# Linear attention and a mixture of experts in fp32: queries and folded projection as further groups of the experts' loop

## The chip, the cores and the metric

One core of a Trainium2 chip runs the kernel. The metric is the device time of one execution in microseconds (us), the median of the runs shown. The engines are PE (TensorE matmuls; PEld is its weight load), DVE (VectorE), ACT (ScalarE), POOL (GpSimd) and SP (SyncE, which here only issues DMAs). PSUM, where matmuls accumulate, has 8 banks of 128 x 512 fp32; SBUF holds tiles of 128 partitions. In the profile, L12 is line 12 of the kernel's own file.

## The reference

2048 tokens x of width D = 512. All weights are fp32. Two branches of the same tokens are mixed by a gate for each token:

```python
phi = lambda t: jnp.where(t > 0, t + 1, jnp.exp(t)) + 1e-6
pq, pk = phi(q), phi(k)                        # q, k, v = x @ wqkv, H = 32 heads of 16
kv = jnp.einsum("bhsd,bhse->bhde", pk, v)      # one 16 x 16 state for each head
z = jnp.einsum("bhsd->bhd", pk)
num = jnp.einsum("bhqd,bhde->bhqe", pq, kv)
den = jnp.einsum("bhqd,bhd->bhq", pq, z)[..., None] + 1e-6
a = (num / den).transpose(0, 2, 1, 3).reshape(B, S, D) @ wo
...
h = _silu(x @ w1[e]) @ w2[e]                   # for each of 8 experts, F = 1792
b = b + w[e] * h                               # w: softmax gates; top 8 of 8, so all
g = sigmoid((x * gate_w).sum(-1, keepdims=True))
out = g * a + (1 - g) * b
```

Nearly all work is the experts' two layers over all tokens.

## The kernel before, in words

**Precision.** Each fp32 product is made of three matmuls in a rounded fp32 format (F32R): `mm3` (L57) multiplies high by high, high by low and low by high. So each operand is split: ACT copies the high part, DVE subtracts to get the low part.

**Seven products.** Both layers of the experts are multiplied as 2 x 2 blocks with 7 block products in place of 8 (`ORDER`, L103: P1, P7, P2, P4, P6, P5, P3). This needs sums of blocks: of the weights (`prep`, L132, steps 0 to 7), of the tokens (`x_sums`, L384, by DVE subtractions) and of the hidden values (`differ`, DVE). The tokens are taken in two halves of 1024.

**Weights.** `m.groups` (L99) lists the groups: half, expert, pair of blocks of F. `load` fetches a group by DMAs on SP's queue; `prep` splits and sums it in steps dealt out over the seven steps of the group ahead of it. In the first half of the tokens, the second layer's weights are prepared too and written to DRAM (`w2stash`), from where both halves read them.

**Attention** (`attention`, L211) stands ahead of the experts' loop.
1. For each tile of 128 tokens: `g_proj` multiplies the tokens by the keys' weights with the gates' columns; ACT and DVE form phi (`g_done`, L353); a DMA on POOL's queue adds phi's rows to one tile in SBUF (`pks`); `y_acc` (L375) accumulates phi(k)^T x over all tokens in four PSUM banks. Since v = x Wv, the state is that sum times Wv. In the last of these tiles the token sums of the second half are made (L384) and written to DRAM (`xstash`), later loaded for the second half by `x_next`.
2. `q_proj` (L480) forms the queries, 12 matmuls for each of 16 blocks of 128 columns by 512 tokens, `state` (L567) the heads' states, `normaliser` (L552) the sums of keys, `fold` (L590) multiplies the state by wo, so that the projection of a query block is one product with the folded weights. `q_sums` (L501), `q_rec` and `q_norm` (L520) divide by the denominators; `a_out` (L534) does the folded projection, 192 matmuls, scales by the token gate and writes the rows to DRAM (`astash`). Twelve query matmuls stand between the last two tiles' `y_acc`.

**The experts' loop** (`experts`, L685). The order is written out by hand: each engine executes in the order in which the code issues, and each step u of the loop issues a share of every stream. `up` (L727) is six matmuls of the first layer, seven steps for a group; `mid` calls `tick` (L898), six matmuls of the second layer for step n = u - LAG, LAG = 44 steps behind; `other` does the splits of hidden values (`high` on ACT, `low_h` on DVE), `differ` and the weights' `prep`. `load_w2` fetches the stashed second-layer weights, 512 KB for two ticks, on SP's queue. `evict` (L875) takes finished PSUM banks, `finish` (L863) multiplies by the token's expert weight and adds it to a sum in DRAM (`acct`) by an accumulating DMA on POOL's queue. Rows of the first half are transposed during the second half (`rows_first`, L929), with the attention's rows added; those of the second half at the end (`turn_some`, `end`), from tiles that `load_tail` and `load_att` fetch on POOL's queue.

Tiles come from pools with tags and numbers of buffers. A new tile waits until the last use of the buffer that it takes is over. Pools that are closed hand their memory to later ones in the same way.

Of the kernel before, what the change touches and what calls it, by code (L numbers as in the profile page):

```python
# [42 lines left out]
def gated_mix_kernel(ctx: ExitStack, tc: tile.TileContext, xT, x, wk, wv, wqkv_q, wo, wm, out):  # L43
# [18 lines left out]
    def act_copy(dst, src):  # L62
        nc.scalar.activation(dst, src, AF.Copy)  # L63
# [7 lines left out]
    m.wgt = const.tile([P, NT, E], F32, name="wgt")  # L71
    m.gat = const.tile([P, NT], F32, name="gat")
    m.mx = const.tile([P, NT], F32, name="mx")
# [7 lines left out]
    m.X = {}  # L81
    for tb, K in ((1, 0), (2, 0), (2, 1), (3, 0), (0, 0), (0, 1), (1, 1), (3, 1)):
        m.X[tb, K] = [x_tile(f"x{tb}{K}{c}", "xs" if (tb, K) == (3, 1) else "x") for c in "hl"]
    m.XO = [[None] * 7, [None] * 7]
    m.xstash = dram.tile([7, 2, P, 2 * TB], F32, name="xstash")
    m.astash = dram.tile([NT, P, D], F32, name="astash")
    m.w2stash = [dram.tile([P, 2, D], F32, name=f"w2stash{i}") for i in range(E * NPAIR * 7 // 2)]
    m.wgtd = dram.tile([E, S], F32, name="wgtd")
    m.acct = dram.tile([2, 2, KT, P, TB], F32, name="acct")

    weights(m)
    attention(m)
    experts(m)

def weights(m):
    nc, v, w1p, act_copy = m.nc, m.v, m.w1p, m.act_copy
    m.groups = [(p, e, q) for p in range(2) for e in range(E) for q in range(NPAIR)]  # L99
    m.NG = len(m.groups)  # L100
    m.NG0 = m.NG // 2
# [7 lines left out]
    def raw_tile(name):  # L109
        return w1p.tile([P, 2048], F32, name=name, tag="rm", bufs=2)  # L110

    def load(g):
        if g >= m.NG:
            return
        p, e, q = m.groups[g]
        src = m.wm[e * NPAIR + q]
        r = raw[g] = raw_tile(f"rm{g}").rearrange("p (r h w f) -> p r h w f", r=2, h=2, w=2)
        for i in range(2):
            nc.sync.dma_start(r[:, i, :, 0, :], src[:, i, :D].rearrange("p (h f) -> p h f", h=2))
        if p == 0:  # L120
            for i in range(2):
                nc.sync.dma_start(r[:, :, i, 1, :], src[:, i, D:].rearrange("p (h f) -> p h f", h=2))
# [9 lines left out]
    def prep(g, step):  # L132
        if g >= m.NG:
            return
        p, e, q = m.groups[g]
        r = raw[g]
        both = p == 0
# [15 lines left out]

        def high2(n, src):
            if both:
                act_copy(two(ws_tile(n), 0), src)

        def low2(n, src, *prods):
            if both:
                w = ws.pop((g, n))  # L160
                v.tensor_sub(two(w, 1), src, f32(two(w, 0)))  # L161
                for half, prod in enumerate(prods):
                    i = (e * 7 + m.ORDER.index(prod)) * NPAIR + q
                    nc.sync.dma_start(m.w2stash[i // 2][:, i % 2].rearrange("p (c f) -> p c f", c=2),
                                      f32(w[:, :, half * HALF:(half + 1) * HALF]))
# [7 lines left out]
        elif step == 1:  # L173
# [6 lines left out]
            high2(1, r[:, :, 1, 1])  # L180
        elif step == 2:
            o = ops[g][6][0]
            v.tensor_sub(o[:, 1], r[:, 1, 1, 0], f32(o[:, 0]))  # L183
            if both:
                w = ws.pop((g, 0))
                v.tensor_sub(w[:, 1, :HALF], r[:, 0, 0, 1], f32(w[:, 0, :HALF]))
                i = (e * 7 + m.ORDER.index("P1")) * NPAIR + q
                nc.sync.dma_start(m.w2stash[i // 2][:, i % 2].rearrange("p (c f) -> p c f", c=2), f32(w[:, :, :HALF]))
        elif step == 3:
            low2(1, r[:, :, 1, 1], "P2", "P4")  # L190
# [6 lines left out]
        elif step == 5:  # L197
            low(5, r[:, 1, :, 0])
            high2(2, r[:, :, 0, 1])
        elif step == 6:  # L200
            low2(2, r[:, :, 0, 1], "P6", "P7")
            high(3, r[:, 0, :, 0], (3, 0), (4, HALF))
            high2(3, r[:, :, 1, 1])
        else:
            low(3, r[:, 0, :, 0])
            low2(3, r[:, :, 1, 1], "P3", "P5")
# [4 lines left out]
def attention(m):  # L211
    nc, tc, v, mm3, act_copy, X, XO = m.nc, m.tc, m.v, m.mm3, m.act_copy, m.X, m.XO
    xT, x, wk, wv, wgt, gat, mx, x_tile = m.xT, m.x, m.wk, m.wv, m.wgt, m.gat, m.mx, m.x_tile
    ctx = ExitStack()
    att = ctx.enter_context(tc.tile_pool(name="att", bufs=1))
    wpool = ctx.enter_context(tc.tile_pool(name="wpool", bufs=4))
    hid = ctx.enter_context(tc.tile_pool(name="hid", bufs=1))
# [14 lines left out]

    def xk(c, tb, k, lo=0, hi=TB):
        return X[tb, k // 2][c][:, k % 2, lo:hi]

    scr = att.tile([P, 8, TB], F32, name="scr")
    yT = scr[:, :KT]
    kvt = scr[:, 7, :].rearrange("p (k f) -> p k f", k=KT)

    zc = att.tile([P, KT, 2, NH], F32R, name="zc")  # L240
    zf = att.tile([P, KT, NH], F32, name="zf")
    mask = att.tile([P, P], F32, name="mask")
    maskh = att.tile([P, KT, NH], F32, name="maskh")
    spread = att.tile([P, KT, P], F32R, name="spread")
    rhs = att.tile([P, 2, TB], F32R, name="rhs")
    pks = att.tile([P, D], F32, name="pks")
    ones = att.tile([P, NH], F32, name="ones")
    lg = att.tile([P, NT, NL], F32, name="lg")

    def sf_tile(name):  # L250
        return hid.tile([P, TB], F32, name=name, tag="sf", bufs=4)


    def hl_tile(name, dt=F32R):
        return hid.tile([P, 2, TB], dt, name=name, tag="hl", bufs=6)

    def o_tile(name):
        return m.w1p.tile([P, 2, TB], F32R, name=name, tag="o", bufs=4)

    def w_tile(name, width=2048):  # L260
        return wpool.tile([P, 8 * G[1]], F32R, name=name, tag="w")[:, :width]
# [4 lines left out]
    def load_raw(name, src):  # L266
        r = m.raw_tile(name)
        nc.sync.dma_start(r, src)
        return four(r)

    raw = {}

    def load_x(tb):
        if tb < 3:
            raw[tb] = load_raw(f"x{tb}", xT[tb])
        else:
            raw[tb] = scr[:, :KT]
            nc.sync.dma_start(raw[tb], four(xT[tb]))

    def split_x(tb, k):  # L280
        split(raw[tb][:, k, :], xk(0, tb, k), xk(1, tb, k))


    g0 = w_tile("g0").rearrange("p (c k f) -> p c k f", c=2, k=KT)
    g1 = w_tile("g1", 8 * G[1]).rearrange("p (c k f) -> p c k f", c=2, k=KT)
    gw = (g0, g1)
    x0 = four(m.raw_tile("x0"))
    r0 = four(m.raw_tile("r0")[:, :KT * G[0]])
    r1 = [hl_tile(f"r1{i}", F32) for i in range(2)]
    for k in range(KT):  # L290
        nc.sync.dma_start(x0[:, k, :], xT[0][:, k * TB:(k + 1) * TB])
        nc.sync.dma_start(r0[:, k, :], wk[:, k * G[0]:(k + 1) * G[0]])
    for i in range(2):
        at = KT * G[0] + 2 * i * G[1]
        nc.sync.dma_start(r1[i][:, :, :G[1]], wk[:, at:at + 2 * G[1]].rearrange("p (k f) -> p k f", k=2))
# [8 lines left out]
    def load_xt(tb):  # L304
        xr[tb] = m.raw_tile(f"xr{tb}").rearrange("p (t d) -> p t d", d=D)
        nc.sync.dma_start(xr[tb], x[tb * TB:(tb + 1) * TB, :].rearrange("(t p) d -> p t d", p=P))

    def split_xt(t):
        xt[t] = o_tile(f"xt{t}")
# [13 lines left out]
    band(maskh, [[P, KT], [-DH, NH]], 1)  # L323
    sp = sf_tile("sp")[:NH, :].rearrange("p (c f) -> p c f", c=KT)
    band(sp, [[P, KT], [1, P]], -DH)
    for i in range(2):
        act_copy(spread[i * NH:(i + 1) * NH], sp)
    for t in (spread, rhs):
        nc.gpsimd.memset(f32(t)[2 * NH:], 0.0)

    def phi(dst, ps):
        nc.scalar.activation(dst, ps, AF.Exp)
        nc.scalar.activation(ps, ps, AF.Relu)
        v.scalar_tensor_tensor(dst, dst, 1.0, ps, op0=ALU.min, op1=ALU.add)

    def eps_high(h, d):
        nc.scalar.activation(h, d, AF.Copy, bias=EPS)  # L340

    def eps_low(lo, d, h):
        v.scalar_tensor_tensor(lo, d, EPS, f32(h), op0=ALU.add, op1=ALU.subtract)
# [9 lines left out]
    def g_done(t, g, ps):  # L353
        if g == 0:
            pk[t] = sf_tile(f"pk{t}"), hl_tile(f"pkh{t}")
            phi(pk[t][0][:, :G[0]], ps)
        else:
            d, h = pk[t]
            phi(d[:, G[0]:], ps[:, :D - G[0]])
            eps_high(h[:, 0], d)  # L360
            eps_low(h[:, 1], d, h[:, 0])
# [22 lines left out]
    def x_sums(p, step):  # L384
        a, b = raw[2 * p], raw[2 * p + 1]
        b11, b21, b12, b22 = a[:, :2], a[:, 2:], b[:, :2], b[:, 2:]
        if step == 0:
            v.tensor_sub(b11, b12, b11)
        elif step == 1:
            v.tensor_sub(b12, b22, b12)  # L390
        elif step == 2:
            v.tensor_sub(b22, b22, b11)
        elif step == 3:
            v.tensor_sub(b21, b21, b22)
        else:
            n, low = divmod(step - 4, 2)
            i, r = ((3, b22), (5, b12), (1, b11), (6, b21))[n]
            if not low:
                if p == 0:
                    XO[0][i] = [x_tile(f"t{i}{c}") for c in "hl"]  # L400
                else:
                    tmp[i] = hl_tile(f"t{i}h"), hl_tile(f"t{i}l")
                act_copy((tmp[i] if p else XO[0][i])[0], r)
            else:
                h, lo = tmp[i] if p else XO[0][i]
                v.tensor_sub(lo, r, f32(h))
                if p:
                    for c, t in enumerate((h, lo)):
                        nc.sync.dma_start(m.xstash[{1: 3, 3: 4, 5: 5, 6: 6}[i], c], f32(t).rearrange("p k t -> p (k t)"))

    tmp = {}

    def x_high(p, n):
# [677 lines left out]
```

## Time and profile before

| | |
|---|---|
| median of 3 runs | 2371.43 us (2370.62 to 2373.01) |
| profiled execution | 2370.8 us |
| its span, first to last instruction | 2369.1 us |
| granted PE clock, mean | 1.000 |
| PE busy | 2347.2 us, 10530 instructions |
| DVE busy | 1783.0 us |
| ACT busy | 1381.8 us |
| POOL busy | 129.6 us |
| DMA | 489.76 MB, mean 207 GB/s |

A busy time is the time in which an engine executed something, and the share is of the span. A chain of waits follows the work back from the last instruction to what released it; an engine with nearly all of this chain is what bounds the kernel. Groups of instructions read "out<-in": the tile written and the tiles read, then the count, busy time, mean ns of one, and the idle time ahead of them with what ended it. Windows give the busy time of each engine in a stretch of the run; a DMA share of 1.00 means that all 16 engines moved data throughout.

### The profile page before, as it was taken

What the parts mean: (1) busy time and instruction counts of PE and PEld (TensorE: products, weight loads), DVE (VectorE), ACT (ScalarE), POOL (GpSimd) and SP (SyncE); (2) the same over time, 40 slices, a digit from 0 to 9 for tenths busy, and PEclk for the clock granted to TensorE, in tenths of its full rate; (3) what the DMA queues carried; (4) which work ended last, traced back from release to release, by engine and by line L of the source; (5) the groups of instructions that cost most, each with busy time, mean ns of one, the idle gap of its engine ahead of it and who ended that gap; (6) DMA issues with size and microseconds to landing.
All of it is one profiled execution on the core that took longest, in us unless ns stands there. A gap on an engine that the chain in (4) does not pass through costs nothing.

```text
span 2369.1 us, 31088 instructions
## 1 busy us (share of the span) xinstructions
PE 2347.2 (99%) x10530; PEld 1939.8 (82%) x10530; DVE 1783.0 (75%) x3023; ACT 1381.8 (58%) x2594; POOL 129.6 (5%) x175
## 2 busy tenths in 40 slices
PE   9999999999999999999999999999999999999998
PEld 8877788888888888888888888888888888888886
DVE  5687888888888888888876667766766667676667
ACT  5556766666666666666655555555555555555553
POOL 2101000000000000000000000000000000000011
PEclk9999999999999999999999999999999999999999
DMA  6626988898888988888894544555454645454456
GB/s 183 212 86 203 307 270 266 265 269 262 270 275 259 285 261 263 271 265 267 270 322 136 157 152 162 165 159 170 143 148 132 165 137 140 150 139 150 139 171 224
DMA packets 297936, 489.76 MB, mean 207 GB/s; under 512 B 22640, under 2 KB 214256, under 8 KB 296880
## 3 DMA queue, kind: packets, MB, share of 16 engines
q1 hardware_dynamic: 278192, 450.99, 57.2%
q0 software_dynamic: 19584, 36.78, 9.2%
q8 instruction: 83, 1.36, 0.2%
q14 instruction: 77, 0.63, 0.1%
HBM read 332.42 MB, written 151.06 MB: 204 GB/s over the span
## 4 chain that ended last, share of the span: by engine, by line
PE 95%; DVE 2%; DMA 2%; ACT 1%; issue 0%; SPq 0%; DVEq 0%; ACTq 0%
PE p L58 15%; PE p L60 15%; PE p L59 15%; PE a L58 9%; PE a L60 9%; PE a L59 9%; PE c L60 4%; PE c L58 4%; PE c L59 4%; PE b L58 2%; PE b L59 2%; PE b L60 2%; PE g L350 1%; PE q L488 1%; PE q L485 1%; PE q L486 1%
## 5 line engine op out<-in xcount | busy, mean ns | idle before, releaser
L58 PE MATMUL p<-ho,w 128*128 128x512 f32 x1568 | 611.2, 390 | 3.6 <-issue 1.8
L60 PE MATMUL p<-ho,w 128*128 128x512 f32 x1568 | 610.1, 389 | 0.0
L59 PE MATMUL p<-ho,w 128*128 128x512 f32 x1568 | 610.0, 389 | 0.0
L836 DVE TENSOR_TENSOR ho<-s,ho 128x512 fp32r<-128x512 f32 x784 | 536.2, 685 | 62.8 <-ACT ho L63 60.5
L63 ACT ACTIVATE ho<-s 128x512 fp32r<-128x512 f32 x784 | 485.7, 621 | 18.0 <-DVE s L817 10.8
L58 PEld LDWEIGHTS p<-ho,w 128*128 128x128 f32 x1568 | 294.3, 188 | 67.2 <-issue 2.2
L60 PEld LDWEIGHTS p<-ho,w 128*128 128x128 f32 x1568 | 294.3, 188 | 61.2
L59 PEld LDWEIGHTS p<-ho,w 128*128 128x128 f32 x1568 | 294.4, 188 | 60.9
L63 ACT ACTIVATE o<-rm 128x512 fp32r<-128x512 f32 x448 | 255.0, 569 | 148.2 <-PE a L60 126.5
L717 ACT ACTIVATE s<-s 128x512 f32<-128x512 f32 x224 | 141.3, 631 | 280.5 <-DVE s L776 207.6
L147 DVE TENSOR_TENSOR o<-rm,o 128x512 fp32r<-128x512 f32 x336 | 230.2, 685 | 16.4 <-ACT o L63 16.1
L776 DVE TENSOR_TENSOR s<-c,s 128x512 f32<-128x512 f32 x112 | 77.3, 690 | 168.1 <-PE c L60 166.2
L63 ACT ACTIVATE ws<-rm 128x512 fp32r<-128x512 f32 (+1 forms) x209 | 117.9, 571 | 65.6 <-DMA w2stash<-ws 54.2
L783 DVE TENSOR_TENSOR s<-a,s 128x512 f32<-128x512 f32 x112 | 77.4, 691 | 73.2 <-PE a L60 72.5
L717 ACT ACTIVATE s<-b 128x512 f32<-128x512 f32 x112 | 67.1, 599 | 110.0 <-PE b L60 96.7
L63 ACT ACTIVATE s<-a 128x512 f32<-128x512 f32 x112 | 66.8, 596 | 93.2 <-PE a L60 93.2
L161 DVE TENSOR_TENSOR ws<-rm,ws 128x512 fp32r<-128x512 f32 x158 | 108.1, 684 | 3.2 <-ACT ws L63 3.2
L183 DVE TENSOR_TENSOR o<-rm,o 128x256 fp32r<-128x256 f32 x112 | 47.1, 421 | 66.0 <-ACT o L63 66.0
L870 POOL DMA_DIRECT2D acct<-c x28 | 24.0, 856 | 1074.9 <-DVE c L866 650.0
L63 ACT ACTIVATE s<-c 128x512 f32<-128x512 f32 x112 | 66.6, 595 | 26.8 <-PE c L60 26.7
L63 ACT ACTIVATE b<-a 128x512 f32<-128x512 f32 x112 | 64.8, 579 | 21.1 <-PE a L60 21.1
L815 DVE TENSOR_TENSOR s<-s,s 128x512 f32<-128x512 f32 x112 | 76.7, 685 | 0.0
(343 smaller groups left out, 4431.9 us busy)
## 6 DMA issues: line engine op xcount, KB each, us to landing
w<-w2stash SPq DMA_DIRECT2D x392, 512.0 KB, 4.3
w2stash<-ws SPq DMA_DIRECT2D x367, 256.0 KB, 4.7
rm<-wm SPq DMA_DIRECT2D x336, 256.0 KB, 4.9
wb<-wgtd SPq DMA_DIRECT2D x16, 512.0 KB, 5.8
acct<-c POOLq DMA_DIRECT2D x28, 256.0 KB, 5.0
acct<-d POOLq DMA_DIRECT2D x28, 256.0 KB, 5.4
acct<-k POOLq DMA_DIRECT2D x26, 256.0 KB, 5.3
acct<-e POOLq DMA_DIRECT2D x26, 256.0 KB, 5.9
```

Of the source, the lines that this page charges most:

```text
L58: nc.tensor.matmul(ps, wh, xh, start=start, stop=False, skip_group_check=True)
L59: nc.tensor.matmul(ps, wh, xl, start=False, stop=False, skip_group_check=True)
L60: nc.tensor.matmul(ps, wlo, xh, start=False, stop=stop, skip_group_check=True)
L63: nc.scalar.activation(dst, src, AF.Copy)
L147: v.tensor_sub(two(o, 1), src, f32(two(o, 0)))
L161: v.tensor_sub(two(w, 1), src, f32(two(w, 0)))
L183: v.tensor_sub(o[:, 1], r[:, 1, 1, 0], f32(o[:, 0]))
L717: nc.scalar.activation(dst, src, AF.Silu)
L776: v.tensor_add(sn[g, 2], bank[g, "c"], sn[g, 2])
L783: v.tensor_add(sn[g, 3], bank[g, "a"], sn[g, 3])
L815: v.tensor_sub(t21, t21, t11)
L836: v.tensor_sub(h[:, 1], s, f32(h[:, 0]))
```

## The change

The queries and the folded projection leave the stage ahead of the loop and become two more "parts" of the loop, one for each half of the tokens, both by 7 products.

- `parts` lists 8 experts and a query part (`e == E`, 2 pairs of blocks) for each half. In the first layer the two halves' query groups (four groups) stand between the first half's and the second half's expert groups; `hidden` (L544) applies phi to their results and writes them to DRAM (`pqd`). In the second layer the query parts come last: 28 further ticks.
- The stage of attention becomes `keys` (L249): keys, `y_acc` and token sums only. The state, the fold, gates and normaliser are done in the first 12 steps of the loop; the folded weights, normaliser and gates go through DRAM.
- The queries are normalised during the second half of the loop, a block of 512 tokens every 49 ticks (`queries_load`, `queries_first`, `queries_last`), in which the token gate is multiplied in.
- Before the query parts, the sums of the experts are loaded from DRAM (`load_sums`, POOL's queue) and the parts' results are added to them by DVE (`evict`); all 16 row tiles are then transposed in the tail. No rows of the attention are stored any more.
- The token sums are made by ACT negating a block in place and a DMA on POOL's queue that accumulates another block onto it, SBUF to SBUF, 512 KB each (`x_sum`). They are spread over tiles 3 to 15. Three split token blocks of the second half are written to DRAM at tile 11 (`x_keep`), and the first group's weights are loaded and prepared at tiles 11 to 15.
- Second-half ticks start 28 steps later than before against the steps of the loop (`LAG1`), so that 28 steps have the first layer alone.

```diff
+    m.parts = [SimpleNamespace(e=e, h=h, n=NPAIR) for h in range(2) for e in range(E)]
+    m.parts += [SimpleNamespace(e=E, h=h, n=2) for h in range(2)]
...
+    for i in (*range(E), 2 * E, 2 * E + 1, *range(E, 2 * E)):
...
-    def x_sums(p, step):
+    def x_sum(p, step):
         a, b = raw[2 * p], raw[2 * p + 1]
         b11, b21, b12, b22 = a[:, :2], a[:, 2:], b[:, :2], b[:, 2:]
-        if step == 0:
-            v.tensor_sub(b11, b12, b11)
...
+        dst, src = ((b11, b12), (b12, b22), (b22, b11), (b21, b22))[step]
+        if step < 3:
+            act_copy(dst, dst, scale=-1.0)
+        nc.gpsimd.dma_start(dst, src, accum_op=ALU.add)
+
+    def x_part(p, i):
...
+        if p == 0:
+            h, lo = XO[0][i] = [m.x_tile(f"t{i}{c}") for c in "hl"]
+        else:
+            both = room(f"t{i}", F32R).rearrange("p (c k f) -> p c k f", c=2, k=2)
+            h, lo = both[:, 0], both[:, 1]
...
+        if p:
+            for c, t in enumerate((h, lo)):
+                nc.sync.dma_start(m.xstash[i, c], f32(t).rearrange("p k t -> p (k t)"))
...
+        if t in (4, 8, 11):
+            load_xt((t + 1) // 4)
...
+        if t in (11, 12):
+            m.load(t - 11)
...
         y_acc(t - 1)
...
+        for p, at in ((0, t), (1, t - 6)):
+            if at in (4, 6, 7):
+                x_sum(p, at // 2 - 1 if at < 7 else 3)
+            if at in (4, 6, 8, 9):
+                x_part(p, {4: 1, 6: 5, 8: 3, 9: 6}[at])
+        if t == 8:
+            x_sum(1, 0)
+        if t == 11:
+            x_keep(0, (2, 0)), x_keep(2, (2, 1)), x_keep(4, (3, 1))
+        if t > 11:
+            m.prep(0, 2 * t - 24), m.prep(0, 2 * t - 23)
     y_acc(NT - 1)
...
+    def hidden(g, f, t, dst, src):
+        part, q = groups[g]
+        if part.e < E:
+            nc.scalar.activation(dst, src, AF.Silu)
+            raw[g, f, t] = dst
+            return
+        if dst is src:
+            dst = r_tile(f"e{g}_{f}{t}")
+        phi(dst, src)
+        nc.sync.dma_start(m.pqd[part.h, t, 2 * q + f], dst)
...
+    LAG = 44
+    LAG1 = LAG + 28
...
+        if part.e == E:
...
+            if prod != "P1":
+                s = sums[part.h, r * 2 + sub, j]
...
+                v.tensor_add(s, src, s)
...
+    def drain():
+        m.yT, m.wvs, m.wos = ([r_tile(f"{n}{k}") for k in range(KT)] for n in ("yT", "wv", "wo"))
+        for k in range(KT):
+            nc.sync.dma_start(m.wvs[k], m.wv[:, k * D:(k + 1) * D])
...
+    def load_sums(h, j):
+        for dt in range(KT):
+            if dt % 2 == 0:
+                r = m.xpool.tile([P, 2, TB], F32, name=f"tl{h}{j}{dt}", tag="x", bufs=14)
+            sums[h, dt, j] = r[:, dt % 2]
+            nc.gpsimd.dma_start(r[:, dt % 2], m.acct[h, j, dt])
...
+        if u == 1:
+            state()
+        if u in (3, 4, 5, 6):
+            fold(u - 3)
...
+        at = n - END
+        if -22 <= at < -14:
+            load_query(0, at + 22)
+        if -8 <= at < 0:
+            load_query(1, at + 8)
+        if at in (-12, -10):
+            load_sums(0, (at + 12) // 2)
+        if at in (3, 5):
+            load_sums(1, (at - 3) // 2)
+        if 11 <= at < 15:
+            rows(0, at - 11)
+        if 16 <= at < 20:
+            rows(0, NTT + at - 16)
+        if 24 <= at < 28:
+            rows(1, at - 24)
```

869 lines of the change are left out of this document (383 added, 486 removed).

## The prediction

> **What bounds the kernel now.** I read the page's busy shares and its chain first, then PE's waits, then the busy time of each engine in stretches of the run.
>
> ```profile
> span 2369.1 us, 31088 instructions
> PE 2347.2 (99%) x10530; PEld 1939.8 (82%) x10530; DVE 1783.0 (75%) x3023; ACT 1381.8 (58%) x2594; POOL 129.6 (5%) x175
> PE 95%; DVE 2%; DMA 2%; ACT 1%; issue 0%; SPq 0%; DVEq 0%; ACTq 0%
> PE a L58 <- ACT hl L63: 3.2, 4, 2.2
> PE a L58 <- ACT s L63: 1.9, 2, 1.2
> ```
>
> PE is busy 99% of the span and carries 95% of the chain. The waits (total us, times, longest) are single events: 3.2 us in the folded projection, which the change removes, and 1.9 us where the loop starts. So a change pays only by fewer PE instructions, and costs wherever PE has to wait. The stretches say where a wait is near (length, then PE, PEld, DVE, ACT, POOL busy, PE clock, share of the 16 DMA engines, GB/s):
>
> ```profile
> 27.00:95.00 68.00, 68.00 (x432) 61.52 (x431) 38.00 (x75) 36.47 (x82) 10.83 (x13) 1.00 0.55 153
> 61.00:64.00 3.00, 3.00 (x26) 2.91 (x25) 2.27 (x5) 2.16 (x5) 0.85 (x1) 1.00 0.49 87
> 97.00:116.00 19.00, 19.00 (x100) 15.41 (x99) 11.79 (x26) 9.42 (x17) 0.62 (x1) 1.00 1.00 358
> 225.00:300.00 75.00, 72.85 (x319) 59.33 (x318) 66.63 (x112) 56.49 (x111) 2.98 (x7) 1.00 0.93 306
> 400.00:600.00 200.00, 200.00 (x884) 165.62 (x883) 168.51 (x280) 128.80 (x245) 7.72 (x9) 1.00 0.86 267
> 2325.00:2334.00 9.00, 9.00 (x41) 7.47 (x40) 5.21 (x9) 3.89 (x7) 0.00 (x0) 1.00 1.02 407
> ```
>
> In the keys' stage (27 to 95 us) PE never waits, with the DMA engines at 0.55. In the first half of the loop (400 to 600) they are at 0.86, DVE at 168.51/200 = 84%. At 97 to 116 us and in the tail, transfers fill them (358 GB/s at 1.00, 407 at 1.02). DMA is the second resource, and this change adds DMA just where it is scarce.
>
> **The change part by part.** The clock is 1.00 throughout, so one row prices a matmul.
>
> ```profile
> 27.10 0.28 PE L350 MATMUL g<-g,x10h 128*128 128x256 f32 x1
> 32.81 0.40 PE L350 MATMUL g<-g,x10h 128*128 128x256 f32 x2
> 95.33 0.39 PE L60 MATMUL y<-pkh,xt 128*128 128x512 f32 x1
> 212.06 0.39 PE L58 MATMUL a<-x00h,o 128*128 128x512 f32 x1
> 1298.02 0.39 PE L58 MATMUL a<-n0h,o 128*128 128x512 f32 x1
> 1317.06 0.39 PE L58 MATMUL a<-n0h,o 128*128 128x512 f32 x1
> 104.02 3.77 PE kv L572 x32
> 107.79 0.81 PE z L555 x8
> 114.22 3.44 PE wp L594 x8
> ```
>
> Two groups of the loop start 1317.06 - 1298.02 = 19.04 us apart and hold 84 matmuls: 0.2267 us each. One token tile of the keys' stage takes 32.81 - 27.10 = 5.71 us.
>
> *A, the arithmetic.* Queries (12 matmuls for each of 16 blocks) and folded projection (192) are 384 matmuls; as 7 products of 8 they are 336, that is 48 x 0.2267 = 10.9 us less. I price the whole stage, since its waits go with it. From the end of the last matmul of tile 14 at 95.56 (95.33 plus one cadence) to the loop at 212.06 are 116.5 us. In its place stand the last tile's 12 matmuls (2.7 us), the state, normaliser and fold (3.77 + 0.81 + 3.44 = 8.0 us) and 336 + 32 + 16 = 384 matmuls x 0.2267 = 87.1 us (the 32 sums over heads and 16 spreads are kept): 97.8. So A = -18.7 us, if nothing waits.
>
> *B, the end of the keys' stage.* Before, tile 15 was covered by query products that PE could do meanwhile, and the six stash copies were issued behind it. Now the queue of SP holds, from tile 10 on, in order: t1 (2 x 512 KB), tokens (1 MB), the first weights (4 x 256 KB), six copies of 512 KB (x_keep, line 439 of the changed kernel), the second weights, t5 (2 x 512 KB), and only then what t3 waits for. These are 12 units of 512 KB and 8 of 256 KB: 16 x 512 KB.
>
> ```profile
> pks<-pk POOLq DMA_DIRECT2D x16, 256.0 KB, 3.3
> xstash<-t3h SPq DMA_DIRECT2D x1, 512.0 KB, 2.7
> xstash<-x20h SPq DMA_DIRECT2D x1, 512.0 KB, 10.7
> xstash<-x31l SPq DMA_DIRECT2D x1, 512.0 KB, 12.5
> x<-xT SPq DMA_DIRECT2D x4, 256.0 KB, 4.3
> w<-w2stash SPq DMA_DIRECT2D x392, 512.0 KB, 4.3
> 97.50 0.32 SPq L409 DMA_DIRECT2D xstash<-t5l  x1
> L340 ACT ACTIVATE pkh<-pk 128x512 fp32r<-128x512 f32 x16 | 10.1, 633 | 9.3 <-DVE pk L337 9.3
> L343 DVE SCALAR_TENSOR_TENSOR pkh<-pk,pkh 128x512 fp32r<-128x512 f32 x16 | 11.1, 692 | 11.2 <-ACT pkh L340 11.2
> L335 ACT ACTIVATE pk<-g 128x256 f32<-128x256 f32 x32 | 12.2, 380 | 20.2 <-issue 9.4 <-PE g L350 9.4 <-ACT t3h L63 0.9
> L63 ACT ACTIVATE xt<-xr 128x512 fp32r<-128x512 f32 x16 | 9.9, 620 | 3.3 <-DMA xr<-x 3.3
> L337 DVE SCALAR_TENSOR_TENSOR pk<-pk,g 128x256 f32<-128x256 f32 x32 | 13.2, 419 | 17.7 <-ACT g L336 17.6
> L63 ACT ACTIVATE t3h<-x 128x1024 fp32r<-128x1024 f32 x1 | 1.0, 1043 | 0.0
> ```
>
> At 407 GB/s at share 1.02, 512 KB hold the engines 1.31 us, at 358 GB/s 1.46 us: 21 to 23.4 us for 16. An accumulation inside SBUF isn't shown at 512 KB; the nearest row is pks (256 KB): around one of them the engines are at 0.49 for 3 us, 1.47 us, so 2.9 us at 512 KB. Two token sums and three pks in that stretch add 5.9 + 4.4. The Trainium skill, DMA: Bandwidth & Descriptors, section Anatomy of one DMA — SWDGE (gpsimd) path, fits 2.0 us plus bytes/436e3 for such a DMA, so by that page the moving part of 512 KB would be an estimated 1.2 us; the row of pks doesn't bear that out, and with it the case is the one called *free* below.
>
> Counted from the start of tile 10 the queue fills at 8.0 us (t1 is ready in tile 11, at 5.71 plus some 2.3 of its ACT and DVE work), so t5 lands at 39.2 to 41.7. ACT takes its work in order: t3h waits for that landing (its room is t5's; x_part, line 421 of the changed kernel), and behind it stand two preparations of the first weights, exp and relu of tile 15 (4 x 0.38), its high part (0.63), its low part on DVE (0.69) and xt: 1.04 + 2 x 0.62 + 1.52 + 0.42 + 0.63 + 0.69, some 6 us with the hand-overs. PE gets tile 15 at 45.3 to 47.7 where it was due at 6 x 5.71 = 34.2: 11 to 13.5 us. xt of tiles 12 to 14 reuse the room of three of the copied tiles, and such copies landed after 10.7 to 12.5 us before; what PE loses there is part of the same queue. I take B = +13. Low end: nothing queues, and tile 15 follows tile 14 with no query product between, 1.3 us of the phi chain and 1.7 of the copies' landing, +3. High end: 358 GB/s and landing latency on top, +17.
>
> *C, the state.* Its weights wv (4 x 256 KB, drain, line 760 of the changed kernel) are loaded into memory that opens with the last matmul of tile 15. PE has only 7 matmuls (1.6 us) before the product at step 1, and 256 KB take 4.3 us to land (row of x<-xT): 2.7 us late, plus four issues on SP of 0.32 us or more each, behind stashes: +4.5, from 2 to 7. Behind the state's first matmul PE's whole queue stands, and ACT and DVE have nothing of the loop to do until it moves.
>
> *D, the first steps of the loop.* Gates, wo, the folded weights' way through DRAM now stand here, and the engines were at 0.93 with 2.15 us of PE idle in 225 to 300. +1 (0 to 5).
>
> *E, the last parts.* 28 more ticks of 1.36 us (6 x 0.2267) each need half a 512 KB load, 0.66 us of the engines. On POOL's queue from the last expert's sixth product on stand 6 accumulations (256 KB, 1.47 us by pks, 1.8 with read and write in DRAM as I estimate it) and 26 loads of 256 KB (0.66): 28 us of work at the 0.7 us per tick that SP's loads leave, 40 ticks. They start near tick 768, so the last lands near 808, and the second half's sums are wanted at tick 800, with some 4 ticks of slack from PSUM. +3 (-1 to +8); the tail before was late too.
>
> *F, the end.* Before, four DVE additions closed the kernel; now copies, shared by ACT and DVE.
>
> ```profile
> 2362.70 2.48 DVE L951 TENSOR_TENSOR at<-o,at 128x512 f32<-128x512 f32 x4 [0.42 <-PE o L957]
> 2342.50 3.10 DVE L836 TENSOR_TENSOR ho<-s,ho 128x512 fp32r<-128x512 f32 x5 [0.78 <-ACT ho L63]
> L717 ACT ACT_TABLE_LOAD x1 | 1.3, 1283 | 0.0
> ```
>
> Half of 2.48, and a bit of the way: -1.5 (-2 to 0).
>
> *G, the four added groups and the queries' blocks.* Three more DVE operations of 0.62 to 0.69 us (3.10/5, row of L343) in a group of 19.04 raise DVE from 84% to 95%; four table switches are 4 x 1.283 = 5.1 us of ACT, which is at 128.80/200 = 64%. PE hides both; if DVE's slack of 3.0 us per group were gone, each further operation would cost 0.69. +0.5 (0 to 2). The Trainium skill, ScalarE: Activation LUTs, section What ACT_TABLE_LOAD costs, adds a drain of about 1.38 us to each, which no row here shows; 10.6 us on ACT by that estimate, hidden as well.
>
> Sum: -18.7 + 13 + 4.5 + 1 + 3 - 1.5 + 0.5 = +1.8 against the profiled run's 2370.8 (span 2369.1 plus 1.7): 2372.6. The median of three is 0.6 above that run: 2373.
>
> **The rivals.** *Forecast, the queue eats the gain:* as worked out, 2373. For it: the keys' stage holds 0.55 x 68 = 37 us of DMA; 8 token sums (23), the six copies (8) and 2 MB of weights (5.6) bring it to 74 us in 68. Own range: B from 8 and the rest at their low sides, -18.7 + 8 + 3 + 0.5 + 1 - 1.5 + 0.3 = -7.4, to B 17, C 6, D 2, E 5, G 1, +10.8: 2364 to 2382.
>
> *Free:* the accumulations cost little and tile 15 only waits for its own chain (B 3, C 2, D 0, E 3). -18.7 + 3 + 2 + 0 + 3 - 1.5 + 0.5 = -11.7; with E at its 1, -13.7: 2357. For it: x stashes landed in 2.7 us when the queue was short (t3h), and the queue of SP has pauses before tile 10. Against: ACT is in order, and 10.7 us of x20h.
>
> *Late sums (the slower side):* POOL's loads of the sums lag SP's weight loads. If its queue gets 0.6 us per tick instead of 0.7, 28 us need 47 ticks, and the last sums land at tick 815; past 800 and 4 of slack, each tick costs 1.36 us: 11 x 1.36 = 15 instead of E's 3: 2385. It decides from tick 804 on. For it: the share is already 1.02 at 2325 to 2334. Against: weights for the last ticks are loaded ahead, which leaves the queue free sooner.
>
> *The change doesn't do what it says:* the 48 matmuls aren't saved or the sums are done on DVE after all. The diff leaves little room: order and counts of products follow from `parts`; then A would be near -7.8 and the time 2384.
>
> **How the numbers follow.** Forecast 0.50, free 0.29, late sums 0.15, the rest 0.06. 0.2% (4.7 us, about what a measurement of this kernel can tell from no change) puts the bounds at 2366.7 and 2376.2. The forecast's range gives 0.05 faster, 0.27 same, 0.18 slower; free is faster; late sums and most of the rest slower: 0.34, 0.28, 0.38. The range 2355 to 2385 leaves out the lower third of free and the upper half of late sums.
>
> **What would show it.** B: waits of ACT for DMA at xt of tiles 12 to 14 and at t3h, PE idle before the last tile's matmuls, and a DMA share near 1 in the 30 us before the loop; A: the loop's second step reached some 18.7 us earlier than 212, plus B. C: PE waiting for wv at the state's 32 matmuls. E: PE waiting for DVE or for the sums in the last 28 ticks. G: no PE waits at the query groups. If ACT never waits for a stash, B is wrong and the time is near 2357; if PE's waits before the loop are over 20 us, B's high end is too low.

## The result, and the profile after

The changed kernel takes 2441.05 us (median of 4 runs, 2438.0 to 2442.8) against 2371.75 us before: a ratio of 1.0291, with a 95% interval from 1.0273 to 1.0309. It is slower by 2.9%, where no change was forecast; none of the rivals reached that far.

Two lines of the changed kernel's page:

```profile
span 2437.3 us, 31414 instructions
PE 2386.7 (98%) x10483; PEld 1940.2 (80%) x10483; DVE 1821.5 (75%) x3099; ACT 1419.3 (58%) x2656; POOL 150.6 (6%) x208
```

There are 47 PE instructions fewer (48 matmuls saved, one transpose more), as counted, and yet PE is *busy* for 39.5 us longer. That cannot be waiting: many instructions take longer. So two things have to be told apart, waits and pace. The waits of PE (total us, times, longest):

```profile
PE y L58 <- ACT xt L63: 15.6, 3, 6.4
PE kv L777 <- DMA wv<-wv: 3.9, 2, 2.9
PE n L879 <- DVE pq L867: 3.7, 4, 0.9
PE n L879 <- DVE az L864: 2.9, 4, 0.7
PE c L58 <- DMA n4h<-xstash: 2.6, 1, 2.6
PE y L58 <- ACT pkh L63: 2.1, 1, 2.1
```

These six rows add up to 30.8 us, of which the three waits of the first are half. They stand before the token products in tiles 6, 13 and 15 of the keys' stage (each product is that of the tile before, and in tile 15 of tile 15 itself). Stretches of the changed kernel (length, then PE, PEld, DVE, ACT, POOL busy with counts, PE clock, DMA share, GB/s):

```profile
44.00:56.00 12.00, 8.11 (x43) 6.81 (x42) 7.70 (x15) 10.05 (x20) 3.44 (x4) 0.86 0.57 103
84.00:100.00 16.00, 10.62 (x53) 9.00 (x52) 4.24 (x8) 6.16 (x14) 1.72 (x2) 0.79 1.04 341
100.00:124.00 24.00, 17.63 (x89) 14.80 (x88) 15.82 (x29) 12.12 (x25) 5.09 (x7) 0.86 1.02 309
124.00:136.00 12.00, 8.06 (x44) 7.13 (x43) 1.88 (x3) 1.72 (x4) 0.00 (x0) 0.85 1.00 312
400.00:600.00 200.00, 200.00 (x869) 162.84 (x869) 167.56 (x277) 125.43 (x237) 10.19 (x12) 1.00 0.87 266
1205.00:1245.00 40.00, 36.13 (x143) 28.31 (x142) 25.85 (x46) 24.05 (x46) 1.71 (x2) 0.91 0.90 335
```

Three things are to be seen. From 84 to 136 us the DMA engines are full (1.00 to 1.04), as the forecast had it. In the stretches with PE's longest waits its granted clock is below 1: the trace has it at one half for 3.4 or 6.8 us at the end of, or soon after, each wait of 2.1 us and more in these six rows. Behind the shorter waits, 1.9 us and less, it stays at 1. And from 400 to 600 us, where PE is busy for all 200 us at clock 1.00, it does 869 matmuls; before, there were 884 in the same stretch, with the same share of the other engines. That is 1.7% slower, in the middle of the first half of the loop, whose matmuls the change left alone.

The rows of the second layer's matmuls, three to a product (count, busy, mean ns of one), show which ones. Before the change:

```profile
L58 PE MATMUL p<-ho,w 128*128 128x512 f32 x1568 | 611.2, 390 | 3.6 <-issue 1.8 <-DVE d L890 0.9 <-DVE k L893 0.7
L60 PE MATMUL p<-ho,w 128*128 128x512 f32 x1568 | 610.1, 389 | 0.0
L59 PE MATMUL p<-ho,w 128*128 128x512 f32 x1568 | 610.0, 389 | 0.0
```

After it:

```profile
L58 PE MATMUL p<-ho,w 128*128 128x512 f32 x1624 | 645.6, 398 | 2.7 <-ACT p L63 1.9 <-DVE d L736 0.5
L60 PE MATMUL p<-ho,w 128*128 128x512 f32 x1624 | 645.3, 397 | 0.0
L59 PE MATMUL p<-ho,w 128*128 128x512 f32 x1624 | 638.9, 393 | 0.0
```

For L58, L59 and L60 in turn these are 398, 393 and 397 ns where there were 390, 389 and 389. The timeline of the changed kernel around 615 us has the starts of both layers' matmuls:

```profile
614.00 0.39 PE L59 MATMUL p<-ho,w 128*128 128x512 f32 x1
614.23 0.40 PE L60 MATMUL p<-ho,w 128*128 128x512 f32 x1
614.47 0.40 PE L58 MATMUL p<-ho,w 128*128 128x512 f32 x1
614.71 0.39 PE L59 MATMUL p<-ho,w 128*128 128x512 f32 x1
614.93 0.40 PE L60 MATMUL p<-ho,w 128*128 128x512 f32 x1
615.17 0.39 PE L58 MATMUL a<-t3h,o 128*128 128x512 f32 x1
615.40 0.39 PE L59 MATMUL a<-t3l,o 128*128 128x512 f32 x1
615.62 0.39 PE L60 MATMUL a<-t3h,o 128*128 128x512 f32 x1
615.85 0.39 PE L58 MATMUL a<-t3h,o 128*128 128x512 f32 x1
616.08 0.39 PE L59 MATMUL a<-t3l,o 128*128 128x512 f32 x1
```

From 614.00 to 615.17 five matmuls of p take 0.234 us each; from 615.17 to 616.08 four of a take 0.2275. Averaged over the trace, from start to start, p takes 233.4 ns and the first layer 227.7, against 226.7 ns for both before.

Where were the first waits? The rows of ACT ahead of each of the three, the first matmul after each, the state's, and where the loop and its ticks start (b, then p):

```profile
43.90 1.06 ACT L63 ACTIVATE x<-x 128x1024 f32<-128x1024 f32 x1 [7.18 <-DMA x<-x]
49.06 0.79 PE L58 MATMUL y<-pkh,xt 128*128 128x512 f32 x1 [3.90 <-ACT xt L63]
95.15 0.63 ACT L63 ACTIVATE xt<-xr 128x512 fp32r<-128x512 f32 x1 [8.53 <-DMA xstash<-x20h]
95.83 0.79 PE L58 MATMUL y<-pkh,xt 128*128 128x512 f32 x1 [5.38 <-ACT xt L63]
112.07 1.06 ACT L63 ACTIVATE t<-x 128x1024 fp32r<-128x1024 f32 x1 [4.53 <-DMA xstash<-t]
118.51 0.80 PE L58 MATMUL y<-pkh,xt 128*128 128x512 f32 x1 [6.37 <-ACT xt L63]
123.82 0.54 PE L559 MATMUL b<-x00h,o 128*128 128x512 f32 x1
128.63 1.13 PE L777 MATMUL kv<-yT,wv 128*128 128x128 f32 x8 [2.88 <-DMA wv<-wv]
204.30 0.39 PE L58 MATMUL p<-ho,w 128*128 128x512 f32 x1
```

The first tick of the kernel before:

```profile
276.67 0.39 PE L58 MATMUL p<-ho,w 128*128 128x512 f32 x1
```

ACT waits for the landing of a token sum (7.18 us, negation of a block), of the copy of x20h (8.53, here xt itself waits) and of t5's copy (4.53), each time with xt at or behind that place in its order, and PE behind xt. The matmul after each wait takes 0.79 us instead of 0.39.

**The accounts.** The spans differ by 2437.3 - 2369.1 = 68.2 us. The loop starts at 123.82, where without waits it would at 98.3 (tile 14 ended at 95.56 before, and tile 15 takes 2.7): the prediction's term B is 25.5. From there to the first tick are 80.5 us; before, 276.67 - 212.06 = 64.6, and 8.0 of state, normaliser and fold came in: C and D are 7.9. A is taken as the prediction has it, -18.7. This leaves 68.2 + 18.7 - 25.5 - 7.9 = 53.5 us in and behind the loop, where the forecast had 2.0 (E, F and G). Of these, the pace of the matmuls should be well over half: the loop's 4872 matmuls of each layer, at 233.4 and 227.7 ns instead of 226.7, are 32.6 + 4.9 = 37.5 by that estimate.

### The profile page after: what moved, and what is told of

Same layout as the page of the kernel before. It is cut to its first block, busy times and chain, and to the rows that moved or that the text cites. A ratio compares the mean times of both kernels' runs of the same rounds, so it can differ in the third digit from the quotient of the medians.

```text
span 2437.3 us, 31414 instructions
## 1 busy us (share of the span) xinstructions
PE 2386.7 (98%) x10483; PEld 1940.2 (80%) x10483; DVE 1821.5 (75%) x3099; ACT 1419.3 (58%) x2656; POOL 150.6 (6%) x208
## 5 line engine op out<-in xcount | busy, mean ns | idle before, releaser
L58 PE MATMUL p<-ho,w 128*128 128x512 f32 x1624 | 645.6, 398 | 2.7 <-ACT p L63 1.9
L60 PE MATMUL p<-ho,w 128*128 128x512 f32 x1624 | 645.3, 397 | 0.0
L59 PE MATMUL p<-ho,w 128*128 128x512 f32 x1624 | 638.9, 393 | 0.0
L671 DVE TENSOR_TENSOR ho<-s,ho 128x512 fp32r<-128x512 f32 x784 | 536.1, 685 | 55.2 <-ACT ho L63 53.5
L58 PEld LDWEIGHTS p<-ho,w 128*128 128x128 f32 x1624 | 305.1, 188 | 76.1 <-ACT p L63 6.6
L60 PEld LDWEIGHTS p<-ho,w 128*128 128x128 f32 x1624 | 304.9, 188 | 74.3
L59 PEld LDWEIGHTS p<-ho,w 128*128 128x128 f32 x1624 | 305.5, 188 | 71.6
L63 ACT ACTIVATE o<-rm 128x512 fp32r<-128x512 f32 x240 | 136.7, 570 | 82.2 <-PE a L60 63.1
L63 ACT ACTIVATE o<-rs 128x512 fp32r<-128x512 f32 x224 | 127.3, 568 | 63.7 <-PE a L60 60.1
L183 DVE TENSOR_TENSOR o<-rs,o 128x512 fp32r<-128x512 f32 x168 | 114.8, 683 | 13.8 <-ACT o L63 13.0
L183 DVE TENSOR_TENSOR o<-rm,o 128x512 fp32r<-128x512 f32 x180 | 123.1, 684 | 1.5 <-ACT o L63 1.4
```

What stands on the lines that cost most here:

```text
L58: nc.tensor.matmul(ps, wh, xh, start=start, stop=False, skip_group_check=True)
L59: nc.tensor.matmul(ps, wh, xl, start=False, stop=False, skip_group_check=True)
L60: nc.tensor.matmul(ps, wlo, xh, start=False, stop=stop, skip_group_check=True)
L63: nc.scalar.activation(dst, src, AF.Copy, scale=scale, bias=bias)
L183: v.tensor_sub(two(o, 1), src, f32(two(o, 0)))
L671: v.tensor_sub(h[:, 1], s, f32(h[:, 0]))
```

## The experiments

**Theories.** The second layer's weight tiles lie, in the kernel before, at a multiple of 128 bytes in each partition (208128), as do all tiles that PE reads in the loop. In the changed kernel, `w2p` is a pool on the right side of SBUF, and its tiles start at 217056, 96 past a multiple of 128. Theory one: the start address slows PE. Rival: the place at the end of the memory, or traffic there. The change names neither; it only moved the pool to where `misc` had been.

### w_aligned: the weight tiles at a multiple of 128

```diff
             misc.close()
+            pad = ctx.enter_context(tc.tile_pool(name="pad", bufs=1, side="right", reuse_waits="tile"))
+            pad.tile([P, 24], F32, name="pad", tag="pad")
             m.w2p = ctx.enter_context(tc.tile_pool(name="w2p", bufs=1, side="right", reuse_waits="tile"))
```

> The changed kernel with the tiles of the second layer's weights 96 bytes lower, at a start that is a multiple of 64 bytes. Theory: such a weight load at a start 32 bytes past a multiple of 64 slows the matmul that runs beside it; the second layer's 4872 matmuls go from 233.4 to 226.8 ns each and the few first-layer ones beside them lose 1 ns, about 37 us: 2404 us. Rival: it is the place at the high end of SBUF, or more traffic there, that slows them; 96 bytes change nothing: 2441 us.

Measured: 2407.8 us, ratio 1.0157 (1.0142 to 1.0172). The stretch from 400 to 600 us:

```profile
400.00:600.00 200.00, 200.00 (x884) 165.62 (x883) 169.86 (x281) 128.31 (x242) 10.21 (x12) 1.00 0.88 268
```

884 matmuls, as before the change, and near the 2404 us of the theory. 33 us of the loss come from 96 bytes of address. The same account as above (loop at 125.8 us, first tick at 205.5, span 2404.1) gives 19 us in and behind the loop for this kernel, 34 less than the 53.5.

### before_w32: the kernel before, its weight tiles moved by 32 bytes

```diff
         if i < 2 * NW:
...
+            if i == 0:
+                hp.tile([P, 8], F32, name="pad", tag="pad")
             w2s[i] = at.tile([P, 2, 2, HALF], F32R, name=f"w2{i}", tag=tag, bufs=bufs)
+            if i == 0:
+                hp.tile([P, 24], F32, name="pad2", tag="pad2")
```

> The kernel before with its second-layer weight tiles 32 bytes higher and nothing else changed in its order. Theory of the start address: 4704 matmuls gain 6.6 ns and the others a little, 31 to 36 us: 2403 to 2408 us. Rival (place or traffic): 2372 us, as before.

Measured: 2406.09 us, ratio 1.0147 (1.0132 to 1.0162), 34.8 us more for 32 bytes:

```profile
400.00:600.00 200.00, 200.00 (x869) 162.83 (x868) 165.31 (x274) 127.17 (x240) 6.87 (x8) 1.00 0.84 262
```

The rival falls: the place is the old one, and the pace is that of the changed kernel, 869.

### w_64 and before_ho32: which multiple, and which operand

`w_64` is w_aligned with 8 in place of 24 in the pad: the weights start 64 past a multiple of 128. `before_ho32` puts the two pads of before_w32 around the tiles of the hidden values `ho` instead of those of the weights.

> The changed kernel with the second layer's weight tiles 32 bytes lower: at a multiple of 64 bytes that is not one of 128. If 64 is what counts, its matmuls stand at 226.8 ns and the time near 2406 us; if 128, they stay slower than 228 ns and the time lies between 2406 and 2441 us.

> The kernel before with the split hidden values (the moving operand of the second layer) 32 bytes higher, the weights as they were; every sixth tile lies elsewhere and stays at a multiple of 64. If only weight loads mind the start address: 2371 us and 226.8 ns throughout. If any read of PE does: 5 in 6 of the second layer's matmuls at 230 to 237 ns, the sixth at 226.8, and 2390 to 2400 us.

Measured in one run each: 2457.49 and 2414.52 us. The two stretches, w_64 first, then before_ho32:

```profile
400.00:600.00 200.00, 200.00 (x863) 161.70 (x862) 166.12 (x275) 124.20 (x236) 11.10 (x13) 1.00 0.87 262
```

```profile
400.00:600.00 200.00, 200.00 (x865) 162.35 (x864) 164.67 (x273) 126.30 (x239) 6.85 (x8) 1.00 0.85 260
```

A start of 64 past is worse than one of 96 or 32, so 64 is not the measure. The moving operand matters as well. Both expectations failed in the time: w_64 lies above both of its ranges, and before_ho32 above its 2390 to 2400. The second failed in kind, too: the matmuls of the sixth tile, whose operands both start at multiples of 128, are as slow (means of 230 to 236 ns, by their place among the six) as the others; in w_64 even first-layer matmuls, which read no w at all, go up to a mean of 235.5 ns at one of their six places. So it isn't that a badly placed read is slow by itself.

### before_all32: everything that PE reads moved alike

```diff
+    const.tile([P, 8], F32, name="pad")
     m.ident = const.tile([P, P], F32, name="ident")
```

> The kernel before with every tile that PE reads moved up by the same 32 bytes (one pad ahead of the first of them), so that all starts agree among each other but none is a multiple of 64. If what counts is the start address by itself: 2404 to 2440 us, matmuls of the loop at 229 ns and more. If what counts is the moving operand's start against the weights' start: 2371 us and 226.7 ns.

Measured in one run: 2375.22 us.

```profile
400.00:600.00 200.00, 200.00 (x884) 165.62 (x883) 168.14 (x278) 128.04 (x242) 6.86 (x8) 1.00 0.86 268
```

884 again, though no tile of the loop starts at a multiple of 64 any more. What counts is how the starts of the tiles that PE reads stand to one another. The 4 us above the kernel before do not come from this stretch; where this one run lost them is open. Worked out from the starts of all matmuls, the median step of 12 matmuls (six of each layer; the mean for before_ho32, where five of six `ho` tiles moved) takes, by the starts modulo 128:

| kernel | x and o | ho | w | step of 12, ns |
|---|---|---|---|---|
| before, w_aligned | 0 | 0 | 0 | 2720 |
| before_all32 | 32 | 32 | 32 | 2720 |
| changed | 0 | 0 | 96 | 2767 |
| before_w32 | 0 | 0 | 32 | 2767 |
| before_ho32 | 0 | 32 | 0 | 2778 |
| w_64 | 0 | 0 | 64 | 2787 |

Three kernels share one value, two share another. One more rival can be settled from the changed kernel's trace: that the two layers' tiles must agree with each other, and not the two operands of one layer. In the last ticks the second layer runs alone; there its matmuls with `w` 96 off still take 234.3 ns from start to start, and 227.3 in the kernel before. Why matmuls with well-placed operands are slowed too stays open; that PE's two streams keep the phase in which one of them was delayed would fit, and is only argued.

### sums_dve: token sums by DVE

```diff
-        dst, src = ((b11, b12), (b12, b22), (b22, b11), (b21, b22))[step]
-        if step < 3:
-            act_copy(dst, dst, scale=-1.0)
-        nc.gpsimd.dma_start(dst, src, accum_op=ALU.add)
+        out, one, two = ((b11, b12, b11), (b12, b22, b12), (b22, b22, b11), (b21, b21, b22))[step]
+        v.tensor_sub(out, one, two)
...
-        if i == 3:
-            act_copy(h, r, scale=-1.0)
-            v.scalar_tensor_tensor(lo, r, -1.0, f32(h), op0=ALU.mult, op1=ALU.subtract)
-        else:
-            split(r, h, lo)
+        split(r, h, lo)
```

> The changed kernel with the token sums as DVE subtractions in the same places, no negation on ACT and no accumulating DMA for them. Theory: PE's wait of 4.1 us in tile 6, and some 2 us of the half clock that follows it, stand on ACT's negation behind the first sum's landing; both go, and 8 sums less in the queue bring tile 15 some 1 to 4 us earlier: 2431 to 2435 us. Rival: the queue of SP is what all three waits stand on, so tile 6's wait is only replaced by DVE's lateness: 2438 to 2442 us.

Measured: 2427.36 us, ratio 1.0237 (1.022 to 1.0254), 13.7 us less than the changed kernel, more than expected. Of PE's waits for xt, 15.6 us in three, this is left:

```profile
PE y L58 <- ACT xt L63: 7.2, 2, 3.7
```

Tile 6 does not wait any more, and tiles 13 and 15 wait 3.7 us and less. By these two traces the accumulations were 8.4 us of waiting; that the other 5 are half clock and late starts is not shown. The wait of tile 6 is not steady: 3.9 us in the changed kernel's trace, 6.3 and 6.5 in those of w_aligned and state_late, which have the same code up to there.

### keep_early: the six copies two tiles earlier

```diff
-        if t == 11:
-            x_keep(0, (2, 0)), x_keep(2, (2, 1)), x_keep(4, (3, 1))
+        if t == 8:
+            x_keep(0, (2, 0)), x_keep(2, (2, 1))
+        if t == 9:
+            x_keep(4, (3, 1))
```

> The changed kernel with the six copies of token blocks to DRAM issued at tiles 8 and 9 instead of 11. Theory: xt of tile 12 no longer waits for their landing, so PE's wait of 5.5 us and 2.3 us of half clock go, and t5's copies land some us earlier, which takes some of the 6.5 us before tile 15: 2428 to 2433 us. Rival: the engines are full at that time anyway, the wait moves to tile 9 to 11 or to t1: 2438 to 2442 us.

Measured: 2433.83 us, ratio 1.0258 (1.0243 to 1.0274), 7.2 us less and 0.8 above the range expected. Its waits:

```profile
PE y L58 <- ACT xt L63: 11.9, 4, 5.8
PE kv L779 <- DMA wv<-wv: 5.2, 1, 5.2
```

Tile 13's wait fell from 5.4 to 0.8 us, as the theory has it, with a new one of 1.0 us in tile 14, and the state's wait for wv grew by 1.3: part of the gain went to the next load in the queue.

### state_late: the state six steps later

```diff
-        if u == 1:
+        if u == 7:
             state()
-        if u in (3, 4, 5, 6):
-            fold(u - 3)
+        if u in (9, 10, 11, 12):
+            fold(u - 9)
...
-        if u == 12:
+        if u == 18:
             misc.close()
```

> The changed kernel with state, fold, normaliser, gates and gate rows six steps later in the loop. Theory: the 4.3 us that PE waits for wv at the state, and the half clock behind it (32 matmuls in 6.5 us where they took 3.8 before), go: 2433 to 2437 us. Rival: PE only meets the next late thing (the tables of phi and silu, DVE's weight sums), nothing is gained: 2440 to 2442 us.

Measured: 2435.21 us, ratio 1.0264 (1.0249 to 1.028), 5.8 us less, as expected. PE's wait for wv is gone from the list.

### all: the edits together

The four edits (w_aligned, sums_dve, keep_early, state_late), a tile of its own for `spread`, and the spread products of the queries' division one step later (`8 <= s` in place of `7 <= s`, and so on).

> The changed kernel with the aligned weight tiles, token sums on DVE, the copies at tiles 8 and 9, the state six steps later, a room of its own for the tile that spreads the denominators (phi of tile 0 waited for its copy), and the queries' division one step later. If the losses add up as single edits show them (33 + 14 + 5 to 7 + 5, some 3 and some 5): 2366 to 2378 us. If they overlap less than that, or what is left is the arithmetic alone, 2357 us, the time that the case called free gave. Above 2380 us a wait has taken the place of those removed.

Measured: 2382.72 us, ratio 1.0049 (1.0037 to 1.0062): above 2380. A wait took the place of those removed. The waits that lead its list:

```profile
PE a L58 <- DVE pq L863: 6.4, 4, 1.6
PE n L875 <- DVE pq L863: 5.7, 4, 1.4
```

The division got worse, by its waits from 6.6 us to 12.1: in each of the four blocks the second of the four products waits 1.4 us for DVE to empty the bank of the first, and the bank of the fourth is still in use when the next group of the loop opens its own (1.6 us a block).

### all2: the division spread out

`all` with the four spread products in steps 9, 14, 16 and 21 of a block, so that DVE empties each bank meanwhile:

```diff
-        elif 7 <= s < 7 + KT:
+        elif s in (9, 14, 16, 21):
+            c = (9, 14, 16, 21).index(s)
```

and two more edits: `y_acc(13)` behind the key products of tile 15, and all tiles of the keys' stage at multiples of 128, rows of 266 columns padded to 288. The tile for `spread`, which had a room of its own in `all`, shares one with others of that stage here.

> The kernel called all with three edits: the division's four spread products not in neighbouring steps but in steps 9, 14, 16 and 21 of the block (in all, PE waited 3.4 us for each of four blocks and more behind it); tile 13's token product moved behind tile 15's key products, to cover phi of tile 15 (PE waited 2.9 us, and the half clock after it); and the key weights' tiles and all others of that stage laid at multiples of 128 bytes, rows of 266 columns padded to 288. Theory: 10 to 13 us of query waits, 4 us before the loop, 2 to 3 us of matmul pitch in the keys' stage (384 key matmuls from 121 ns to 114 or 118): 2363 to 2368 us, faster than the kernel before. Rival: the stall before tile 15 and in the divisions are replaced by others, and padding does nothing: 2375 to 2383 us.

Measured: 2367.22 us over 11 runs, ratio 0.9983 (0.9974 to 0.9992): faster than the kernel before by 4 us. Of the 15.5 us below `all`, 12.1 are the division's waits; no wait of a for pq and none of n is left. Of the two other edits nothing is to be seen: PE's wait before tile 15 is as long as in `all`, and the key matmuls of 256 and 266 columns stand at 119.4 and 123.0 ns from start to start (117.4 and 123.4 in `all`).

```profile
PE y L58 <- ACT xt L63: 2.7, 1, 2.7
```

### all3 and all3_accum: two more waits, and the accumulation alone

`all3` drops those two edits, puts two preparation steps behind phi of tile 15 on ACT, and loads the second half's token blocks up to two steps earlier (`x_next(3)` and `x_next(4)` at k = 5 and 6). `all3_accum` is `all3` with the token sums of the changed kernel.

> The kernel called all2 without the later product of tile 13 and without the padding of the keys' weights (neither did anything there), and with two edits: steps 4 and 5 of the first group's preparation behind phi of tile 15 on ACT instead of ahead of it (they held ACT for some 3.3 us while PE waited 2.8), and the second half's token blocks loaded up to two steps earlier (the fifth landed 3 us late while the engines were at 0.73 before). Theory: both waits and the half clock behind them go, 4 and 4 to 5 us: 2357 to 2360 us, clearly faster than before. Rival: the blocks' loads wait for PE on SP's queue and hold up the weights behind them, or tile 15 meets the next thing: 2365 to 2370 us.

> The kernel called all3 with the token sums again by ACT's negation and the accumulating DMA, as in the changed kernel. If the accumulation itself costs, by ACT standing behind its landing: the wait of 4 to 6 us in tile 6 and its half clock come back, and one before tile 13 or 15: 8 to 14 us over all3. If it only hurt because the queues were full: within 2 us of all3.

Measured: all3 2367.22 us, ratio 0.9981 (0.9971 to 0.999); all3_accum 2378.48 us, ratio 1.0031 (1.002 to 1.0041). In all3 two waits for xt at tile 15 are 0.8 us together, where one of 2.7 stood, but nothing was gained:

```profile
PE c L58 <- ACT s L63: 2.7, 1, 2.7
PE p L58 <- DMA w<-w2stash: 2.0, 2, 1.5
PE y L58 <- ACT xt L63: 0.8, 2, 0.6
```

The second row is new: the second layer's weights now come late, behind the token blocks that are loaded earlier on SP's queue. The time is the rival's, and this row is what it names. The accumulation costs 11.3 us even in the mended kernel, with tile 6's wait back:

```profile
PE y L58 <- ACT xt L63: 9.7, 4, 6.0
```

## Why the prediction was wrong

**The pace of the loop: +33 us, not in the sum at all.** The prediction priced a matmul by one row ("0.2267 us each") and carried that price into the changed loop because the clock was 1.00 throughout. That step failed. The clock did stay at 1.00 from 136 us on to the transition, and the matmuls still took 1.7% longer, by the start of one pool's tiles: 2767 ns instead of 2720 for a step of 12. w_aligned took 33 us away and before_w32 put 35 into the old kernel. The prediction named no rival in which unchanged matmuls change their pace. The Trainium skill, SBUF — State Buffer, section Operand start alignment, asks that an operand starts at a multiple of its element size and says that this is about legality and not about speed; all starts here obey it, and the runs show a price that the section leaves untimed.

**B, the end of the keys' stage: right in kind, half the size.** The queue did what was forecast (share 1.02 to 1.04), ACT did wait in its order for the copies of x20h (8.53 us) and of t5 (4.53), and PE for xt. But it was 25.5 us for 13, and past the high end of 17. The two waits behind the full queue, 5.4 and 6.4 us, are 11.8, close to the 13. Three terms were missing. One is the wait in tile 6 (3.9 us), far ahead of the full queue: a negation on ACT waits for the landing of the sum before it, which POOL issues only behind the accumulations of pks. The second is a wait of 2.1 us for pkh near the stage's start (0.2 to 2.4 in the other traces with the same code there). The third is the clock: behind each of these three waits for xt, 3.9 to 6.4 us long, PE worked on at half the clock for 3.4 to 5.6 us, so that each cost nearly half as much again, 6.7 us in all.

```profile
core 0: 2437.3 us, clock 0.993
```

At a mean of 0.993, 0.007 x 2437 = 17 us were withheld over the whole run, the pauses' own share included. The Trainium skill, TensorE: Matmul & The Clock Gate, section Part 1: The HAM clock gate (the "warmup" mystery), says that an idle window of about 3.4 us halves the clock until a busy one has passed. The trace agrees on the length: the half-clock stretches last 3.4 or 6.8 us. It asks for less than a whole idle window, though: 2.6 us of waiting, for n4h, were enough here. The prediction had waits priced by their length alone.

**C and D: 7.9 for 5.5.** Right in kind: the state waits for wv (3.9 us for C's 4.5), and state_late takes that away for 5.8 us.

**A: not isolated by any run.** The count is right, 47 PE instructions fewer. all2, with the pace mended and most waits gone, is 74 us below the changed kernel and 4 below the one before, far less than 18.7. By the same account its loop starts at 101.2 us and its first tick at 176.3, so that B is 2.9 and C and D are 2.4 there; with A at -18.7 this leaves 10.4 us in and behind its loop, of which the late blocks n4h and n4l and the half clock behind them are 6.6. What is left over, some 4 us, may belong to A or to the loop.

**G: +0.5 forecast, the second largest miss of a term.** In w_aligned, where the pace is mended, 19 us stand where E, F and G had 2.0, and E and F are not among them, as said below. Shares of DVE and ACT were read, and bank use was not. In the changed kernel the division's products wait 3.7 us for DVE's emptying of one PSUM bank and 2.9 for the denominators that DVE splits, in four blocks; all2 shows the cure. And the token blocks of the second half arrive late (n4h and n4l, 3.2 us, with a half clock after it: 0.91 on the mean from 1205 to 1245 us) while the engines are at 0.90: the transition was taken for free. Before the change PE waited for none of these blocks; no run separates which of the transfers there made them late. These two make some 13 us, and the rest of G stays open.

**E and F: both smaller than forecast.** In the last 137 us PE's waits add up to 2.1 us, for ACT and DVE, where the tail before had 3.7; none is for a load of sums. So E's +3 was not paid; its 1.8 us for an accumulation in DRAM was an extension of the pks row that no run here tests. The end behind the last tick is 0.4 us shorter, not 1.5. The rival of the late sums did not come, and neither did *free*: with the accumulations alone back, all3_accum shows them at 11 us, not at 0.

## What to carry to other kernels

Before pricing unchanged instructions at their old duration, compare the addresses of the tiles that they read: a pool that moves can cost more than the work that the change saves, and a step's period in a steady stretch (884 against 869 matmuls in 200 us) shows it at once. Price a wait of PE of some microseconds by its length plus half of the half-clock stretch that follows it. And an operation on an in-order engine that waits for a DMA's landing is charged to everything behind it: eight accumulating DMAs that spare DVE some 1.2 us each cost 11 us here.

## What the runs showed of the hardware

- PE's pace depends on how the start addresses of moving tiles and weight tiles stand to each other modulo 128 bytes: 226.7 ns for a matmul of 512 columns when they agree (at 0 or all at 32), 230.6 on average with weights 32 or 96 off, 232.2 with 64 off, 231.5 with five of six moving tiles of one layer 32 off.
- This carries over to matmuls of the same step whose own operands agree: in the changed kernel first-layer matmuls take 231.0 ns at the first of their six places and 228.4 at the last.
- A DMA that adds 512 KB within SBUF took 5.5 us from issue to landing (median of 8). One that ran alone, issued at 54.11 us, landed after 4.5 us and kept the engines busy for 0.92 x 3.00 = 2.76 us, close to the 2.9 of the forecast: the engine time was priced rightly, and ACT's wait for the landing was not priced. On POOL's queue they stood behind the accumulations of pks, which made them later still.

```profile
x<-x POOLq DMA_DIRECT2D x8, 512.0 KB, 5.5
55.50:58.50 3.00, 3.00 (x19) 2.63 (x18) 1.35 (x4) 1.69 (x6) 0.48 (x1) 1.00 0.92 175
```
